# Denominators of the first five tiles of the second pass on POOL, during the second group of G; the other tiles' 1e-6 on ACT

## The chip, the cores and the metric

The kernel runs on one core of one Trainium2 chip. A core has five engines with a queue of instructions each: PE (matrix products and transposes), DVE (vector), ACT (activation functions, copies), POOL (GpSimd) and SP (which here only issues DMAs). Each works off its own queue in order, and an instruction waits at the head of its queue until what it needs is there. The metric is the device time of one execution in microseconds (us), the median of several. Before the change it is 804.62 us (three runs, 804.2 to 806.26).

## The reference

Two layers, each a Fourier mixing sublayer and then a linear attention block, over x of 2048 tokens by 640 features in f32. The input generator stores the DFT matrices, wqkv (640 x 1920) and wo (640 x 640). The part that the change touches is the attention. In the names used below, with 32 heads of 20 features and phi a positive feature map:

```
xn   = layernorm(x)
pq   = phi(xn @ wq);  pk = phi(xn @ wk);  v = xn @ wv
kv_h = sum over tokens of pk_h^T v_h          (20 x 20 for each head)
z_h  = sum over tokens of pk_h                (20 for each head)
o_h  = (pq_h @ kv_h) / (pq_h . z_h + 1e-6)
x    = x + concat(o_h) @ wo
```

`pq_h . z_h + 1e-6` is one number for each token and head, the denominator: 32 for each token, 128 x 32 for a tile of 128 tokens.

## The kernel before

x stays in SBUF as 16 tiles X of 128 tokens by 640 features. Products that need more precision than one fast pass are split: `split` makes a high part (a cast on ACT, L134) and a low part (a subtraction on DVE, L135), and PE adds three products.

Attention runs in two passes over the tokens. The first is `keys_values`. For each tile it normalizes x (`norm`, DVE, L128 or L124), transposes it, and computes keys pk and queries pq with phi on ACT (L284 to L286) and DVE (L287). POOL adds up all keys in `pksum` (L299). The values are never computed for each token: instead G = sum of xn^T pk (640 x 640, only the parts needed) is gathered in PSUM, and kv follows as wv^T G. G is gathered in two groups of tokens, tiles 0 to 9 and, after all keys are there, tiles 10 to 15 (`CUT` is 10). For each tile `gram_ready` norms x again, and splits xn and pk (two casts on ACT, two low parts on DVE); the low part of the keys is called w in the trace, that of xn t. `gram` then runs 30 products (L252), five of which share a chunk of features: high times high, high times low, low times high. Work of tile n+1 is made ready while PE is at tile n.

After the first tile of the second group, `total` (L360) multiplies pksum with a matrix of ones on PE, which leaves z, summed over all tokens and copied to all 128 partitions, in spare columns of G's banks. In the kernel before, `total_out` copies z to SBUF (`zb`, three copies on ACT, L369 and L370) when the whole second group is done. In layer 0 the same stage runs pieces of a check that compares loaded constants (DVE, L1047 and L1064, called junk); in layer 1 there are none.

`combine` adds both groups of G (L350, DVE), computes kv (L400), masks it (L409), and multiplies each of six blocks of kv by wo (`rows`, L168 on PE), which gives the matrix M of the second pass. In the same stretch the first tiles of the second pass are prepared: `weigh(n)` multiplies pq and zb on POOL (L444, 128x640) and `weighted(n)` finishes on DVE: a reduction over the 20 features of each head (L457), + 1e-6 (L458), the reciprocal (L459), and pq times the reciprocal in two instructions (L461 with 600 columns, L467 with 40).

`outputs` is the second pass. For each tile n of `order2`: POOL multiplies for tile n+3, five transposes (L140) for tile n+1, `weighted` for tile n+2, 60 products with M (L168), the split of the next tile's transposed weighted queries (L134, L135), and the residual (L500, DVE). In layer 0 this pass also feeds the next layer's Fourier sublayer, tile by tile: statistics and norms on ACT (L112, L113, L126) with scalars on POOL (L114, L115, L118), and folds of tokens on POOL (L748, L749, L753) and DVE (L764 and on). In layer 1 it stores the output instead.

Temporaries of 128 x 640 come from a pool of 12 buffers (`temp`), PSUM has four buffers of two banks. The order of instructions on each engine is set at build time by a scheduler that takes priorities, which the table `AHEAD` moves for named pieces ('0weigh0' is tile 0's `weighted` in layer 0). What waits for what is then fixed; the order in which instructions stand in each queue is part of the program. The engine orders of the two kernels differ only from the second group of G to the end of the second pass in each layer, on PE, DVE, ACT and POOL; SP's order is the same.

Of the kernel before, what the change touches and what calls it, by code (L numbers as in the profile page):

```python
# [8 lines left out]
F32 = mybir.dt.float32  # L9
F32R = mybir.dt.float32r  # L10
AF = mybir.ActivationFunctionType
ALU = mybir.AluOpType
AX = mybir.AxisListType

S, D, H, DH = 2048, 640, 32, 20
# [30 lines left out]
VLOWS = (0, 0, 1, 0)  # L46
WLOWS = ((5, 2), (1, 1))
GATE = 2
AHEAD = {'0out00': -60, '2keep00': -60, '2out10': -600, '1q13': 60, '2keep01': 600, '2keep02': 5, '0kv0': 5, '2out02': -20, '0out10': -600, '0keep00': -5, '1q14': 60, '0w1': 5, '2out01': 20, '0kv2': -600, '0m1': -5, '0kv5': 60, '1weigh15': -20, '0out12': -200, '1res13': 5, '2m1': -20, '0keep10': 60, '0weigh0': 60, '0first': -5, '2out12': -200, '2weigh1': 5, '2first': 60, '0m3': 20, '2out13': -200}


class K:
    def __init__(self, tc, ctx):
        self.tc, self.nc = tc, tc.nc
        nc = self.nc
        self.n = self.layer = self.part = 0
        self.cst = ctx.enter_context(tc.tile_pool(name="cst", bufs=1))
        self.psp = ctx.enter_context(tc.tile_pool(name="ps", bufs=4, space=bass.MemoryType.PSUM))
        self.ident = self.cst.tile([128, 128], F32, name="ident")
        make_identity(nc, self.ident)  # L60
        self.ones = self.cst.tile([128, 128], F32, name="ones")
        nc.vector.memset(self.ones, 1.0)
        self.mhalf = self.cst.tile([128, 1], F32, name="mhalf")
        nc.vector.memset(self.mhalf, -0.5)

# [89 lines left out]
def h2(t):  # L155
    return t.rearrange("p (a b) -> p a b", a=2)
# [16 lines left out]
class Attention:  # L173
    def __init__(self, k, X, order, order2, wqkv, wo, mask, saved=None):
        self.k, self.X, self.order, self.order2, self.mask, self.saved = k, X, order, order2, mask, saved
        self.wqkv, self.wo, self.W = wqkv, wo, {}
        self.kept = {}

    def wt(self):
        return self.k.wp.tile([128, 640], F32R, tag="w", name=self.k.nm("w"))  # L180
# [83 lines left out]
    def keys_values(self, check=None, keep=1, saves=()):  # L264

        saves = list(saves)
        k, nc, W = self.k, self.k.nc, self.W
        pksum = k.temp()
        nc.gpsimd.memset(pksum, 0.0)
        self.PQ, late = {}, []  # L270
        if check is not None:
            check.fetch()

        def proj(part, x, mid=None):
            pu = k.psum()
            for cs in (range(ND),) if mid is None else (range(2), range(2, ND)):
                product(nc, pu, *x, [w[0] for w in W[part]], [w[1] for w in W[part]], cs=cs)
                if mid is not None and cs[0] == 0:
                    mid()
            return pu  # L280

        def phi(pu, out):
            e = k.temp()
            nc.scalar.activation(h2(e), halves(pu), AF.Relu, scale=-1.0)  # L284
            nc.scalar.activation(h2(out), halves(pu), AF.Relu)
            nc.scalar.activation(e, e, AF.Exp, scale=-1.0)  # L286
            nc.vector.scalar_tensor_tensor(out, e, 1e-6, out, op0=ALU.add, op1=ALU.add)  # L287

        x, acc, tail = self.x0, [], None
        for a, b in ((0, CUT), (CUT, NT)):  # L290
            pks = []
            for n in range(a, b):
                with k.ahead("normed", n + 1):
                    xn = self.normed(n + 1) if n + 1 < NT else None
                pk = self.slot()
                pu = proj(1, x)
                with k.ahead("key", n):
                    phi(pu, pk)
                nc.gpsimd.tensor_tensor(pksum, pksum, pk, op=ALU.add)  # L299
                pks.append(pk)  # L300
                def chunks(xn=xn, n=n):
                    tp = k.transposed(xn)
                    with k.ahead("chunks", n):
                        return k.split_chunks(tp)

                def query(i=self.order[n], x=x, mid=None):
                    pq = k.pqp.tile([128, D], F32, tag="pq", name=k.nm("pq"))
                    pu = proj(0, x, mid)
                    with k.ahead("query", i):
                        phi(pu, pq)  # L310
                    self.PQ[i] = pq

                got = []
                if xn is not None and n:
                    got.append(chunks())
                if n < NT - keep:
                    query(mid=None if got or xn is None else lambda: got.append(chunks()))
                else:
                    late.append(query)
                if n in SAVES[0] and saves:  # L320
                    self.save(*saves.pop(0))
                if check is not None and n in STEPS[0]:
                    check.step(True)
                if n == b - 2:
                    with k.ahead("gram", a):
                        ready = self.gram_ready(a, pks[0])
                if xn is not None:
                    x = got[0]
            G = [k.psum() for _ in range(3)]
            tail = tail or k.psum()  # L330
            for n in range(a, b):
                with k.ahead("gram", n + 1):
                    nxt = self.gram_ready(n + 1, pks[n + 1 - a]) if n + 1 < b else None
                self.gram(G + [tail], ready, n == a, n == b - 1, a == 0)
                if n in SAVES[1] and saves:
                    self.save(*saves.pop(0))
                if n == CUT:
                    self.total(G, pksum)
                if check is not None and n in STEPS[1]:
                    check.step(n != STEPS[1][-1])  # L340
                ready = nxt
            if a == 0:
                acc = [self.slot() for _ in range(ND)]
                for c in range(ND):
                    (nc.scalar.copy if c % 2 else nc.vector.tensor_copy)(acc[c][:, :GA], self.place(G, c, 0))
                nc.scalar.copy(acc[ND - 1][:, GA:], self.place(G, ND - 1, 1))
        assert not saves
        self.total_out(G)
        for c in range(ND):
            nc.vector.tensor_tensor(acc[c][:, :GA], acc[c][:, :GA], self.place(G, c, 0), op=ALU.add)  # L350
        c = ND - 1
        nc.vector.tensor_tensor(acc[c][:, GA:], acc[c][:, GA:], self.place(G, c, 1), op=ALU.add)
        for c in range(ND - 1):
            nc.scalar.copy(acc[c][:, GA:], self.place([None] * 3 + [tail], c, 1))
        self.combine(acc, late)
# [16 lines left out]
    def combine(self, G, late):  # L372
# [65 lines left out]
            self.M.append(m)  # L438
        self.next, self.t1 = qd, self.weigh(2)

    def weigh(self, n):
        k = self.k
        t1 = k.temp()
        k.nc.gpsimd.tensor_tensor(t1, self.PQ[self.order2[n]], self.zb, op=ALU.mult)  # L444
        return t1

    def weighted(self, n, t1):

        k, nc, pq = self.k, self.k.nc, self.PQ[self.order2[n]]
        heads = lambda t: t.rearrange("p (h d) -> p h d", d=DH)
        den, rden = (
            k.sm.tile([128, H], F32, tag="sm" + n, name=k.nm(n), bufs=2) for n in ("den", "rden")
        )
        nc.vector.tensor_reduce(den, heads(t1), axis=AX.X, op=ALU.add)  # L457
        nc.vector.tensor_scalar(den, den, 1e-6, None, op0=ALU.add)  # L458
        nc.vector.reciprocal(rden, den)  # L459
        chunks = t1.rearrange("p (i c) -> p i c", i=ND)  # L460
        nc.vector.tensor_tensor(  # L461
            chunks[:, :, :EC].rearrange("p i (h d) -> p i h d", d=DH),
            pq[:, : EC * ND].rearrange("p (i h d) -> p i h d", i=ND, d=DH),
            rden[:, : 6 * ND].rearrange("p (i h) -> p i h", i=ND).unsqueeze(3).to_broadcast([128, ND, 6, DH]),
            op=ALU.mult,
        )
        nc.vector.tensor_tensor(  # L467
            chunks[:, :, EC:].rearrange("p i (h s) -> p h i s", h=2),
            pq[:, EC * ND :].rearrange("p (h i s) -> p h i s", h=2, i=ND),
            rden[:, 6 * ND :].unsqueeze(2).unsqueeze(3).to_broadcast([128, 2, ND, 4]),  # L470
            op=ALU.mult,
        )
        return t1

    def outputs(self, after, between=lambda: None):
# [4 lines left out]
        for n, i in enumerate(self.order2):  # L480
# [16 lines left out]
            for pu, hs in zip(pus, parts):  # L497
# [3 lines left out]
                after(i, hs[0], hs[-1] + 1)  # L501
            if n == NT - GATE:
                late = last
# [854 lines left out]
```

## Time and profile before

| | us |
|---|---|
| median of three runs | 804.62 (804.2 to 806.26) |
| the profiled execution | 805.39 |
| its span, first to last instruction | 803.5 |
| mean granted TensorE clock | 0.992 |

The stages that the change touches, in the profiled execution, from busy time by stage:

| stage | layer 0 | layer 1 |
|---|---|---|
| second group of G, from the total on | 293.27 to 316.55 | 677.40 to 699.10 |
| kv, rows of M, first tiles weighed | 316.55 to 365.00 | 699.10 to 724.85 |
| outputs | 365.00 to 422.60 | 724.85 to 803.50 |

The first stage of layer 0 begins with the total (to 294.65), that of layer 1 after it. In layer 0 the transposes and products of the first tiles of the second pass run within the second stage.

How to read the rows: a row of the timeline is start, length, engine, line, operation, output, inputs, shape and count, and in brackets the idle time before it and what ended it. A group row has busy time of all, the mean of one in ns, and the idle time before. A wait row is who waited for whom: us in total, times, longest. PEld is PE's loading of weights beside its products. Line numbers are those of the kernel before; in the changed kernel the same lines stand some lines further down (L252 becomes L255, L135 becomes L138, L168 becomes L171).

### The profile page before, as it was taken

The page shows a single profiled execution, that of the slowest core. Times are in us where ns is not written, and L with a number is a line of the kernel's source. Part 1 is how long each engine was busy: PE and PEld are TensorE (multiplying, and loading weights), DVE is VectorE, ACT ScalarE, POOL GpSimd, SP SyncE. Part 2 cuts the span into 40 slices and gives each one's busy share as a digit, 9 for nine tenths or more (in the row PEclk, how much of TensorE's full clock was granted, in tenths as well). Part 3 has the DMA queues.
Part 4 walks back from the last instruction along what each step waited for, and adds up shares of the span by engine and source line. Part 5 has one row for each costly group of instructions (what it writes and reads, how often), then busy time and mean ns, then how long its engine had stood idle before and what let it go on. Part 6 is the DMA issues. An engine that isn't in the chain of part 4 may idle for free.

```text
span 803.5 us, 12981 instructions
## 1 busy us (share of the span) xinstructions
PE 744.2 (93%) x4920; PEld 706.5 (88%) x4920; DVE 612.6 (76%) x1153; ACT 337.7 (42%) x592; POOL 317.7 (40%) x354
## 2 busy tenths in 40 slices
PE   0579999999999999999898999999999999999997
PEld 0138899999999999899784899999999999989997
DVE  7799883778774775989978787377896398499982
ACT  4534544545324553455552434445532455341110
POOL 4987991111021111369894756111101111134310
PEclk9989999999999999999999999999999999999999
DMA  9122430455770452000004551044444044001121
GB/s 329 57 86 66 134 101 1 143 162 175 215 229 15 153 179 78 21 1 2 0 1 145 202 204 48 1 142 142 142 142 141 1 142 144 20 12 50 66 84 70
DMA packets 36008, 81.25 MB, mean 101 GB/s; under 512 B 4142, under 2 KB 5937, under 8 KB 35936
## 3 DMA queue, kind: packets, MB, share of 16 engines
q1 hardware_dynamic: 35904, 80.27, 30.9%
q8 instruction: 41, 0.67, 0.3%
q14 instruction: 31, 0.25, 0.1%
q0 software_dynamic: 32, 0.06, 0.0%
HBM read 68.10 MB, written 11.80 MB: 99 GB/s over the span
## 4 chain that ended last, share of the span: by engine, by line
PE 64%; DVE 21%; POOL 5%; DMA 3%; ACT 3%; issue 3%; SPq 0%; DVEq 0%; POOLq 0%; ACTq 0%
PE ps L168 44%; PE ps L252 13%; PE ps L140 3%; PE ps L947 3%; DVE w L135 2%; DVE t L135 2%; DVE junk L1064 1%; DMA ck<-in_ck 1%; DVE x L974 1%; DVE den L457 1%; POOL ab L623 1%; DVE t L461 1%; PE ps L400 1%; DMA rawc<-in_so 1%; DMA x<-in_x 1%
## 5 line engine op out<-in xcount | busy, mean ns | idle before, releaser
L168 PE MATMUL ps<-w,t 128*128 128x320 f32 x2880 | 440.2, 311 | 7.7 <-DVE t L135 5.7
L168 PEld LDWEIGHTS ps<-w,t 128*128 128x128 f32 x2880 | 422.8, 188 | 10.9 <-DVE t L135 7.7
L299 POOL TENSOR_TENSOR t<-t,s 128x640 f32<-128x640 f32 x32 | 58.3, 1822 | 219.3 <-DVE s L287 211.8
L252 PE MATMUL ps<-t,t 128*128 128x256 f32 (+1 forms) x640 | 139.9, 309 | 0.0
L284 ACT ACTIVATE t<-ps 128x640 f32<-128x640 f32 x64 | 45.2, 705 | 156.3 <-PE ps L168 156.3
L252 PEld LDWEIGHTS ps<-t,t 128*128 128x128 f32 x640 | 107.3, 188 | 0.0
L1064 DVE CUSTOM_DVE_ANT_0 junk<-ck,ck 128x688 bf16<-128x688 f32 (+4 forms) x138 | 98.6, 714 | 7.3 <-DMA ck<-in_ck 5.5
L252 PE MATMUL ps<-w,t 128*128 128x384 f32 (+1 forms) x320 | 98.7, 310 | 0.7 <-DVE w L135 0.6
L444 POOL TENSOR_TENSOR t<-pq,t 128x640 f32<-128x640 f32 x32 | 56.1, 1758 | 101.3 <-ACT t L370 48.5
L135 DVE TENSOR_TENSOR t<-ps,t 128x640 fp32r<-128x640 f32 (+1 forms) x66 | 53.8, 817 | 41.3 <-ACT t L134 41.0
L134 ACT CAST t<-ps 128x640 fp32r<-128x640 f32 (+1 forms) x66 | 45.6, 692 | 67.3 <-PE ps L140 63.1
L902 PE MATMUL ps<-cw,ab 128*107 128x512 f32 (+4 forms) x108 | 42.8, 533 | 33.0 <-DVE ab L643 26.1
L287 DVE SCALAR_TENSOR_TENSOR pq<-t,pq 128x640 f32<-128x640 f32 x32 | 27.6, 861 | 54.3 <-ACT t L286 54.3
L902 PEld LDWEIGHTS ps<-cw,ab 128*107 128x107 f32 (+1 forms) x108 | 18.5, 183 | 51.8 <-issue 47.7
L252 PEld LDWEIGHTS ps<-w,t 128*128 128x128 f32 x320 | 60.1, 188 | 1.5 <-DVE w L135 1.5
L947 PE MATMUL ps<-t,u 107*128 107x322 f32 (+1 forms) x306 | 48.9, 315 | 2.6 <-DVE t L135 1.4
L947 PEld LDWEIGHTS ps<-t,u 107*128 107x128 f32 (+1 forms) x306 | 45.8, 189 | 5.0 <-DVE u L928 2.2
L286 ACT ACTIVATE t<-t 128x640 f32<-128x640 f32 x64 | 48.0, 750 | 0.0
L140 PE MATMUL ps<-ident,t 128*128 128x128 f32 x320 | 45.6, 273 | 1.5 <-DVE t L467 1.0
L128 DVE TENSOR_SCALAR t<-x,kept 128x640 f32<-128x640 f32 x58 | 44.4, 766 | 0.7 <-PE ps L252 0.7
L140 PEld LDWEIGHTS ps<-ident,t 128*128 128x128 f32 x320 | 38.3, 140 | 3.2 <-issue 1.5
L134 ACT CAST t<-t 128x640 fp32r<-128x640 f32 x32 | 23.3, 729 | 36.6 <-DVE t L128 31.8
(178 smaller groups left out, 999.4 us busy)
## 6 DMA issues: line engine op xcount, KB each, us to landing
ck<-in_ck SPq DMA_DIRECT2D x48, 346.0 KB
ck<-in_ck SPq DMA_DIRECT2D x48, 344.0 KB
save<-w SPq DMA_DIRECT2D x20, 320.0 KB
w<-save SPq DMA_DIRECT2D x20, 320.0 KB
x<-in_x SPq DMA_DIRECT2D x16, 320.0 KB
out<-x SPq DMA_DIRECT2D x15, 320.0 KB
raw<-in_wqkv SPq DMA_DIRECT2D x10, 320.0 KB
s<-in_wqkv SPq DMA_DIRECT2D x10, 320.0 KB
```

Source lines behind the costliest of these rows:

```text
L134: self.nc.scalar.copy(hi, src)
L135: self.engine(pool).tensor_tensor(lo, src, hi.bitcast(F32), op=ALU.subtract)
L140: self.nc.tensor.transpose(tp[:, 128 * c : 128 * c + 128], src[:, 128 * c : 128 * c + 128], self.ident)
L168: nc.tensor.matmul(pu[:m, 512 * h : 512 * h + HD], s, w[:, HD * h : HD * h + HD], start=first, stop=last)
L252: nc.tensor.matmul(self.place(G, c, part), x[:, 128 * c : 128 * c + 128], p[:, f : f + n], start=start and i == 0, stop=stop and i == 2, s ...
L284: nc.scalar.activation(h2(e), halves(pu), AF.Relu, scale=-1.0)
L286: nc.scalar.activation(e, e, AF.Exp, scale=-1.0)
L299: nc.gpsimd.tensor_tensor(pksum, pksum, pk, op=ALU.add)
L444: k.nc.gpsimd.tensor_tensor(t1, self.PQ[self.order2[n]], self.zb, op=ALU.mult)
L902: nc.tensor.matmul(pu[:m, o : o + n], e, w[:, f : f + n], start=g == 0 and i == 0, stop=g == end and not more and i == len(both) - 1,)
L947: self.k.nc.tensor.matmul(po[:, o : o + 322], s[:m, f : f + 128], w[:m, x, :], start=first, stop=last)
L1064: i = nc.vector.tensor_tensor_reduce(k.junk[:, : a.shape[1]], b, a, 1.0, 0.0, op0, op1, o)
```

## The change

Four things are done. A constant tile of 1e-6 is made. `total_out` is called directly after `total`, within the second group, and no longer after it. `denominators` follows it: for the first five tiles of the second pass (whose queries are all there) POOL multiplies pq and zb, sums the 20 products of each head by four additions that halve the columns (10, 5, 2, 1) and a last one of columns 0 and 4, and adds 1e-6: seven instructions a tile, 35 a layer, in two temporaries by turns and one tile for the 5 x 32 results. `weigh` gives those tiles only a temporary, and `weighted` starts with the reciprocal. For the eleven other tiles the reduction stays on DVE and 1e-6 is added by ACT.

```diff
+EARLY = 5
...
+        self.eps = self.cst.tile([128, 1], F32, name="eps")
+        nc.vector.memset(self.eps, 1e-6)
...
                 if n == CUT:
                     self.total(G, pksum)
+                    self.total_out(G)
+                    self.denominators()
...
         assert not saves
-        self.total_out(G)
...
+    def denominators(self):
+
+        k, nc = self.k, self.k.nc
+        t1 = [k.temp() for _ in range(2)]
+        all_den = k.sm.tile([128, H * EARLY], F32, tag="early", name=k.nm("early"), bufs=1)
+        for n in range(EARLY):
+            if self.order2[n] in self.PQ:
+                self.early(n, all_den[:, H * n : H * n + H], t1[n % 2])
+
+    def early(self, n, den, t1):
+        k, nc = self.k, self.k.nc
+        nc.gpsimd.tensor_tensor(t1, self.PQ[self.order2[n]], self.zb, op=ALU.mult)
+        self.den[n] = den
+        t = t1.rearrange("p (h d) -> p h d", d=DH)
+        for w, o in ((10, 10), (5, 5), (2, 2), (1, 1)):
+            nc.gpsimd.tensor_tensor(t[:, :, :w], t[:, :, :w], t[:, :, o : o + w], op=ALU.add)
+        nc.gpsimd.tensor_tensor(den, t[:, :, 0], t[:, :, 4], op=ALU.add)
+        nc.gpsimd.tensor_scalar(den, den, 1e-6, None, op0=ALU.add)
+
     def weigh(self, n):
         k = self.k
         t1 = k.temp()
+        if n in self.den:
+            return t1
         k.nc.gpsimd.tensor_tensor(t1, self.PQ[self.order2[n]], self.zb, op=ALU.mult)
         return t1
...
-        nc.vector.tensor_reduce(den, heads(t1), axis=AX.X, op=ALU.add)
-        nc.vector.tensor_scalar(den, den, 1e-6, None, op0=ALU.add)
+        if n in self.den:
+            den = self.den[n]
+        else:
+            nc.vector.tensor_reduce(den, heads(t1), axis=AX.X, op=ALU.add)
+            nc.scalar.activation(den, den, AF.Identity, bias=k.eps)
         nc.vector.reciprocal(rden, den)
```

In the changed order on DVE the reciprocals of tiles 0 and 1 stand among the splits of tiles 14 and 15 of the second group, and those of tile 2 ahead of the additions of G. On POOL the instructions of tiles 0 and 1 alternate, then those of 2 and 3, then tile 4's follow; tile 2's product stands ahead of tile 1's last addition. On PE twelve short products of tile 11 now stand ahead of the total.

More of the change, by code (lines that the diff above doesn't have):

```diff
@@ L176, in __init__ @@
         self.wqkv, self.wo, self.W = wqkv, wo, {}
-        self.kept = {}
+        self.kept, self.den = {}, {}
     def wt(self):
```

## The prediction

> **What bounds the kernel now.** I read the page first, then the chain of waits around the second group of G, then busy time by stage, then the groups by line.
>
> ```profile
> span 803.5 us, 12981 instructions
> PE 744.2 (93%) x4920; PEld 706.5 (88%) x4920; DVE 612.6 (76%) x1153; ACT 337.7 (42%) x592; POOL 317.7 (40%) x354
> PE 64%; DVE 21%; POOL 5%; DMA 3%; ACT 3%; issue 3%; SPq 0%; DVEq 0%; POOLq 0%; ACTq 0%
> ```
>
> PE is busy 93% of the span, so only places where PE waits can pay, and every new PE wait costs. The chain, layer 0, over the stage that the change fills (start, length, work):
>
> ```profile
> 291.21 2.01 POOL t L299
> 293.22 0.04 issue
> 293.27 1.38 PE ps L360 x10
> 294.65 21.90 PE ps L252 x149
> 316.55 4.41 PE ps L168 x30
> ```
>
> The last sum of keys on POOL releases the total, then PE runs the 150 products of tiles 11 to 15 of the second group (4.38 us a tile) without a gap. The stages (window and length; then busy us of PE, PEld, DVE, ACT, POOL):
>
> ```profile
> 293.27:316.55 23.28, 23.28 (x161) 23.28 (x162) 14.06 (x27) 9.02 (x18) 0.00 (x0) 1.00 0.25 76
> 335.64:365.00 29.36, 29.26 (x205) 29.01 (x205) 26.96 (x46) 14.52 (x30) 19.06 (x27) 1.00 0.03 9
> 365.00:422.60 57.60, 51.55 (x348) 48.96 (x346) 51.16 (x75) 30.44 (x61) 52.31 (x71) 1.00 0.01 2
> 677.40:699.10 21.70, 21.70 (x151) 21.70 (x149) 9.92 (x15) 8.46 (x17) 0.00 (x0) 1.00 0.20 60
> 699.10:724.85 25.75, 24.00 (x177) 21.53 (x176) 25.73 (x51) 10.11 (x21) 12.03 (x7) 1.00 0.05 10
> 724.85:803.50 78.65, 73.05 (x516) 72.70 (x514) 60.00 (x96) 9.72 (x14) 16.00 (x10) 0.98 0.18 69
> ```
>
> In G (rows 1 and 4) PE is full and POOL is idle: that is the room the change uses. In layer 0's outputs (row 3) PE idles 6.05 us with DVE and POOL both near 90%. In layer 1's outputs (last row) PE sets the pace.
>
> **Part 1: 35 POOL instructions in each G.** Prices, from the groups by line (busy in all, mean ns):
>
> ```profile
> L444 POOL TENSOR_TENSOR t<-pq,t 128x640 f32<-128x640 f32 x32 | 56.1, 1758 | 101.3 <-ACT t L370 48.5 <-PE ps L168 26.9 <-DVE w L135 6.4
> 385.54 0.18 POOL L749 COPY ab<-t 128x2 f32<-128x2 f32 x1
> 385.68 0.87 POOL L753 TENSOR_TENSOR ab<-t 128x319 f32<-128x319 f32 x1
> L791 POOL TENSOR_TENSOR ab<-ab,ab 128x640 f32<-128x640 f32 x3 | 4.7, 1568 | 0.1
> ```
>
> 640 elements take 1.57 us undisturbed, 319 take 0.87, two take 0.18: (1.57 − 0.87)/321 = 2.2 ns an element over 0.17. The adds of 320, 160, 64 and 32 elements, and the last of 32, then take 0.87, 0.52, 0.31, 0.25 and 0.25, the 1e-6 0.19; with the product 1.57 that is 3.96 us a tile and 20 us a layer. No row has adds of this stride (20 apart). The bounds: 0.17 each, the part that does not grow with the size (1.5 less for each tile), and twice the price (2.4 more). I take the single price, which all four rows above support for f32 operands of their sizes.
>
> 20 us would fit under 21.9 if POOL ran beside DVE. It does not, and this is the step that decides:
>
> ```profile
> 290.98 0.82 DVE L135 TENSOR_TENSOR t<-t,t 128x640 fp32r<-128x640 f32 x1
> 291.21 2.00 POOL L299 TENSOR_TENSOR t<-t,s 128x640 f32<-128x640 f32 x1 [6.58 <-DVE s L287]
> 291.72 1.85 DVE L128 TENSOR_SCALAR t<-x,kept 128x640 f32<-128x640 f32 x1
> 295.16 0.61 DVE L128 TENSOR_SCALAR t<-x,kept 128x640 f32<-128x640 f32 x1
> ```
>
> The POOL product that started inside a DVE split took 2.00 instead of 1.57 (it ended 1.41 after the split), and the norm behind it took 1.85 where one with POOL idle takes 0.61: each waits for the other's whole instruction. What DVE has to do in G is just of that kind:
>
> ```profile
> L135 DVE TENSOR_TENSOR t<-t,t 128x640 fp32r<-128x640 f32 x32 | 26.3, 821 | 12.7 <-ACT t L134 12.2
> 296.66 0.87 DVE L1064 CUSTOM_DVE_ANT_0 junk<-ck,ck 128x692 bf16<-128x692 f32 x1
> 301.95 0.70 DVE L1064 CUSTOM_DVE_ANT_0 junk<-ck,ck 128x519 bf16<-128x519 f32 x1
> 303.83 0.33 DVE L1064 CUSTOM_DVE_ANT_0 junk<-ck,ck 128x173 bf16<-128x173 f32 x1
> 304.78 0.82 DVE L135 TENSOR_TENSOR t<-t,t 128x640 fp32r<-128x640 f32 x1 [0.62 <-ACT t L134]
> 305.53 0.82 DVE L135 TENSOR_TENSOR w<-s,t 128x640 fp32r<-128x640 f32 x1
> L369 ACT COPY t<-ps 128x256 f32<-128x256 f32 x4 | 1.6, 411 | 0.0
> ```
>
> Splits follow each other 0.75 apart (304.78, 305.53), 0.07 under what one lasts, and I take as much off the norm and the check pieces. I write t(n) and w(n) for the low parts of tile n's norm and keys, x(n) for its norm. In the new order PE does twelve products of tile 11 before the total (256 columns each, so some 1.4 us, under 12 × 0.147). They start when w(11) lands, which follows POOL's last sum (ended 293.22) and takes 0.74: 293.95. The total (1.38) then ends near 296.75, and ACT's copies of z, which follow it bank by bank (0.41, 0.41 and a shorter one), near 297.2. The splits of tile 12 on ACT stand behind these copies. Alone that is a delay of 0.8 us. From 297.2 on POOL runs. Up to w(14) and with it the new DVE order has six splits (t and w of tiles 12, 13 and 14: 4.5 us), x(13) and x(14) (1.1), five check pieces in layer 0 (three at 0.80, then 0.63 and 0.26: 3.3) and the reciprocals of early tiles 0 and 1. These two wait for POOL, which interleaves tiles 0 and 1 and slips in tile 2's product: 3 × 1.57 + 2 × 2.39 = 9.5. One after the other: 297.2 + 8.9 + 9.5 + 0.4 for the reciprocals and 0.5 for hops from ACT (0.62 at 304.78) = 316.5 for w(14), where PE wants it at 316.55 − 2 × 4.38 = 307.8. Then two tiles of PE: G ends at 325.3, **+8.7** at strict alternation. In layer 1 there are no check pieces. Z lands 2.55 after the stage's start, as in layer 0 (297.2 after 294.65), at 680.0; DVE has 5.6 and the first reciprocal's 0.2, POOL 9.3: w(14) at 695.1, wanted at 699.10 − 8.76 = 690.3: **+4.8**.
>
> Alternation is not quite strict. A stretch of layer 0's outputs with both busy:
>
> ```profile
> 384.09 0.77 DVE L461 TENSOR_TENSOR t<-pq,rden 128x600 f32<-128x600 f32 x1
> ...
> 387.89 0.83 DVE L766 TENSOR_TENSOR ab<-ab,ab 128x640 f32<-128x640 f32 x1
> 387.99 1.44 POOL L753 TENSOR_TENSOR ab<-t 128x319 f32<-128x319 f32 x1
> ```
>
> Between 384.09 and 389.43 twelve operations, 6.4 us at undisturbed prices, pass in 5.3: 0.1 saved a handoff. With two handoffs for each of thirteen DVE operations up to w(14) in layer 0 and of eight in layer 1: 8.7 − 2.6 = **+6.1**, 4.8 − 1.6 = **+3.2**. Bounds: +0.8 and +0.3 when DVE's slack (w(15) was ready at 306.35, five microseconds early) swallows the rest, +13.5 when strict.
>
> By the Trainium skill ("SBUF — State Buffer", section "SBUF: two separate sides"), the port pair that VectorE and GpSimd share is an exclusive lock, held for a whole instruction when VectorE reads two SBUF inputs or runs a two-port mode, and the loser fully blocks. The trace agrees in kind (1.85 against 0.61), and by that rule the strict sum would hold.
>
> **Part 2: what outputs get back.** DVE loses the addition of all sixteen tiles (eleven go to ACT) and the reduction of five:
>
> ```profile
> L457 DVE TENSOR_REDUCE den<-t 128x32 f32<-128x640 f32 x32 | 25.6, 804 | 0.6 <-POOL t L444 0.6
> L458 DVE TENSOR_SCALAR den<-den 128x32 f32<-128x32 f32 x7 | 3.6, 521 | 0.0
> 384.01 0.15 DVE L458 TENSOR_SCALAR den<-den 128x32 f32<-128x32 f32 x1
> PE ps L168 <- DVE t L135: 4.8, 4, 2.1
> PE ps L168 <- ACT t L134: 1.0, 2, 0.7
> 724.12 0.73 PE L140 MATMUL ps<-ident,t 128*128 128x128 f32 x5 [0.96 <-DVE t L467]
> ```
>
> Row 2 is the stage from 365 to 422.6 of layer 0: seven additions, 3.6 us, of which 0.15 each is work (row 3) and the rest waiting for POOL. That waiting goes partly to the next instruction (the product, which waits for POOL too). So between 1.0 and 3.6, and never above PE's idle 5.8 (rows 4 and 5); POOL, at 52.31 of 57.60, also limits it. I take −2.4. The stage before, with the early tiles 3 and 4, has PE at 29.26 of 29.36: nothing. In the stage of the products of rows I take −0.4 in layer 0, half of one reduction (0.80), since the early tiles' reductions there are gone and PE runs nearly without a gap; in layer 1 the wait at 724.12, −0.7 of 0.96. Layer 1's outputs: nothing, DVE has 18 us to spare. Sum **−3.5** (0 to −6.5).
>
> ACT's addition is one more hop.
>
> ```profile
> ACT t L126 <- POOL mv L118: 13.0, 7, 3.0
> L112 ACT ACTIVATION_READ_ACCUMULATOR t<-x 128x1 f32 x17 | 3.2, 187 | 0.0
> ```
>
> Nothing on ACT has its size; a read of one element takes 0.19 (row 2), a copy of 256 columns 0.41 (above), so 0.2 to 0.4, and DVE's queue has another tile's instruction between reduction and reciprocal, which covers it; uncovered it would be 0.4 a tile on a chain that has slack in layer 1 and none in the stage from 365. It can also be late where it stands behind a statistic that waits for POOL (row 1). Seven waits, up to 3.0: in the new order the additions of tiles 8, 9, 11 and 12 stand behind one. Zero taken, up to +3 for the range. The memset of 1e-6 runs at the start beside loads: nothing. SP's queue keeps its order.
>
> The rest of part 1: two temporaries are held through G, so ACT's query of the late tile waits for tile 3's adds and a mask for tile 4's; the reciprocal of tile 2 stands ahead of G's additions and waits for POOL to about 297.2 + 16 + 10.5 = 323.7, before 325.3: covered by the same delay.
>
> **Sum** on the profiled execution, 805.39: +6.1 + 3.2 − 3.5 = +5.8, so 811.2; against the median 804.62 (0.77 lower) **810.5**.
>
> **Rivals.** *DVE's slack holds* (the other side). Place: w(14) of both layers. If POOL's short adds let DVE pass at once, DVE waits mostly for pieces of 0.2 to 0.5 and G is late by 0.8 to 3 in all, while outputs give 3.5 to 6.5: 799.5 to 804, 802 as its middle. It decides once G's two delays sum to under 3.5. For it: DVE is 14.06 busy of 23.28 in G, and 5 us early. Against: the reciprocals in DVE's queue make w(14) wait for POOL's whole two trees, whichever engine is served first. *Strict alternation*: no handoff saves anything, G costs +13.5: 805.39 + 10.0 − 0.77 = 814.6. For it: the norm's 1.85; against: the twelve operations in 5.3. *Strided adds cost twice.* Each tree is 2.4 us dearer, two of them ahead of w(14), twice: +8 to +9, 819. For it: no row has them. Against: rows of POOL go by element count. *The ACT addition is late* behind the waiting statistics: part 2's −2.4 goes and up to 3 comes: 814 to 816. *The denominators are not done within G*: 20 us of POOL after 297.2 do not fit before 316.55 with DVE's 11 in between; but what then waits (tile 2's reciprocal, above) lands within the delay already counted, so it gives the forecast.
>
> **How the numbers follow.** Forecast (with the last rival) 0.42, 810.5, own range 806 to 815; strict alternation 0.10; slack holds 0.30; adds twice 0.10; late addition 0.08. No change is within 0.3%, 802.2 to 807.0, about what a measurement tells. Slack splits 0.17 faster and 0.13 same; the forecast leaves 0.05 same. So faster 0.17, same 0.18, slower 0.65. The range leaves out the best of the slack and the worst of doubled adds: 801.5 to 818.
>
> **What would show it.** In the new profile: POOL busy about 20 us in each second group of G; x(13), x(14) and the splits there at 1.2 to 2.3 instead of 0.61 and 0.82; PE waiting in L255's products for w(14) or the splits; G's last product about 6 later in layer 0 than before, counted from the total, and 3 later in layer 1. In the outputs PE's waits for the low split falling from 4.8 to 2 to 3, the wait at 724.12 gone. I am wrong if G shows no PE wait, if the adds take over 1.5 times their price, or if PE waits in the outputs grow.

## The result, and the profile after

The changed kernel takes 812.26 us (median of four runs, 811.15 to 814.65) against 804.72 us for the kernel before (four runs): a ratio of 1.0095, 95% interval 1.0083 to 1.0107. It is slower, 1.8 us above the 810.5 forecast and inside its range of 801.5 to 818. The profiled execution is the fastest of the four, 811.15 us with a span of 809.4, and that of the kernel before lies 0.7 above its median. So the profiles, from which all stages below are taken, show 5.9 us of the 7.5 by which the medians differ.

The page of the changed kernel: the span, busy time of the engines, and the chain of waits by engine.

```profile
span 809.4 us, 13016 instructions
PE 746.8 (92%) x4920; PEld 708.0 (87%) x4920; DVE 602.6 (74%) x1112; ACT 344.1 (43%) x614; POOL 358.8 (44%) x414
PE 63%; DVE 18%; POOL 11%; ACT 3%; issue 3%; DMA 1%; SPq 0%; ACTq 0%; POOLq 0%; DVEq 0%
```

DVE has 10.0 us less to do, POOL 41.1 more (two layers of 20), and POOL's share of the chain went from 5% to 11%. The chain of waits of the changed kernel in layer 0, around the second group of G (start, length, work) shows where; some steps marked "issue", all under 0.3 us, are left out:

```profile
291.35 2.00 POOL t L302
293.35 3.83 issue
...
297.22 3.66 POOL t L456 x2
300.88 7.69 POOL t L460 x8
308.57 0.99 POOL early L461 x2
309.63 0.33 POOL early L462
309.99 0.04 DVE rden L487
310.26 1.56 DVE junk L1092
311.82 0.01 DVE cm L1092
311.82 0.77 DVE t L138
312.59 0.07 DVE rden L487
312.78 1.90 DVE w L138
314.72 8.46 PE ps L255 x56
323.19 4.40 PE ps L171 x30
```

Before, that stretch of the chain was PE alone: 150 products without a gap. Now it runs through POOL's products and adds (L456, L460 to L462) for 12.7 us, a reciprocal (L487), a check piece, and the low parts t(14) and w(14) on DVE; only then come PE's last 56 products of G. Z was in SBUF at 297.2, as worked out; w(14) landed at 314.7 (worked out at strict alternation: 316.5). PE's four waits in that group, from the timeline of the changed kernel, are for w(11), w(12), w(13) and w(14):

```profile
294.09 0.40 PE L255 MATMUL ps<-w,t 128*128 128x256 f32 x1 [1.20 <-DVE w L138]
301.62 0.39 PE L255 MATMUL ps<-w,t 128*128 128x256 f32 x1 [1.15 <-DVE w L138]
307.99 0.39 PE L255 MATMUL ps<-w,t 128*128 128x256 f32 x1 [1.61 <-DVE w L138]
314.72 0.39 PE L255 MATMUL ps<-w,t 128*128 128x256 f32 x1 [2.10 <-DVE w L138]
```

Busy time by stage of the changed kernel (window, length, then PE, PEld, DVE, ACT, POOL): the second group of layer 0 and that of layer 1.

```profile
293.35:323.19 29.84, 24.24 (x161) 23.26 (x162) 23.19 (x33) 8.67 (x18) 25.32 (x31) 1.00 0.16 47
679.99:706.30 26.31, 24.13 (x161) 23.20 (x162) 18.55 (x21) 8.64 (x18) 21.96 (x28) 1.00 0.18 54
```

DVE and POOL together show 48.5 us busy in 29.84 us of layer 0's G: as the stretched instructions below show, the busy time of both contains time in which one waits for the other.

To place the difference I cut each execution at the same events: the start of POOL's last sum of keys, the first product of the rows of M, the residual (L500 before, L528 after) of the first tile, that of the last tile. Busy time by stage between these cuts, for the rows of M and for the outputs of layer 0, first before, then after:

```profile
316.39:341.71 25.32, 23.92 (x178) 22.01 (x177) 25.05 (x53) 10.83 (x22) 11.58 (x6) 1.00 0.09 21
341.71:424.94 83.23, 75.65 (x514) 72.66 (x513) 73.70 (x114) 44.85 (x89) 70.54 (x97) 1.00 0.03 9
```

```profile
323.02:346.97 23.95, 22.96 (x175) 21.34 (x174) 19.28 (x40) 11.03 (x22) 6.14 (x7) 1.00 0.14 34
346.97:430.46 83.49, 78.24 (x518) 74.99 (x517) 68.92 (x99) 47.67 (x100) 73.38 (x97) 0.98 0.03 10
```

| stage, us | before | after | difference |
|---|---|---|---|
| start to POOL's last sum, layer 0 | 291.21 | 291.35 | +0.14 |
| G, layer 0 | 25.18 | 31.67 | +6.49 |
| rows of M and first products, layer 0 | 25.32 | 23.95 | −1.37 |
| outputs, first to last residual, layer 0 | 83.23 | 83.49 | +0.26 |
| Fourier and first pass of layer 1 | 249.02 | 247.52 | −1.50 |
| G, layer 1 | 25.14 | 28.16 | +3.02 |
| the rest of layer 1 | 104.40 | 103.26 | −1.14 |
| span | 803.5 | 809.4 | +5.9 |

A residual is an instruction of DVE, so the number of products that PE has done by the first one varies: 178 before, 175 after, and 170 to 185 in the experiments. A product is worth 0.147 us (75.65 for 514), so the rows of M and the outputs should be read together or by PE's idle time, which is the length less PE's busy time.

### The profile page after: what moved, and what is told of

It reads as the page before. It is cut to its first block, busy times and chain, and to the rows that moved or that the text cites. A ratio compares the mean times of both kernels' runs of the same rounds, so it can differ in the third digit from the quotient of the medians.

```text
span 809.4 us, 13016 instructions
## 1 busy us (share of the span) xinstructions
PE 746.8 (92%) x4920; PEld 708.0 (87%) x4920; DVE 602.6 (74%) x1112; ACT 344.1 (43%) x614; POOL 358.8 (44%) x414
## 4 chain that ended last, share of the span: by engine, by line
PE 63%; DVE 18%; POOL 11%; ACT 3%; issue 3%; DMA 1%; SPq 0%; ACTq 0%; POOLq 0%; DVEq 0%
PE ps L171 42%; PE ps L255 11%; PE ps L143 3%; PE ps L975 3%; DVE t L138 2%; POOL t L460 2%; PE ps L404 1%; PE ps L930 1%; POOL ab L651 1%; DVE x L1002 1%; DVE junk L1092 1%; DVE w L138 1%; POOL t L456 1%; ACT t L137 1%; DVE t L131 1%
## 5 line engine op out<-in xcount | busy, mean ns | idle before, releaser
L1092 DVE CUSTOM_DVE_ANT_0 junk<-ck,ck 128x688 bf16<-128x688 f32 (+4 forms) x138 | 100.7, 730 | 5.6 <-DMA ck<-in_ck 3.9
L469 POOL TENSOR_TENSOR t<-pq,t 128x640 f32<-128x640 f32 x22 | 35.1, 1598 | 63.1 <-PE ps L171 33.5
L138 DVE TENSOR_TENSOR t<-t,t 128x640 fp32r<-128x640 f32 x32 | 30.3, 947 | 17.2 <-ACT t L137 17.0
```

Source lines behind the costliest of these rows:

```text
L138: self.engine(pool).tensor_tensor(lo, src, hi.bitcast(F32), op=ALU.subtract)
L1092: i = nc.vector.tensor_tensor_reduce(k.junk[:, : a.shape[1]], b, a, 1.0, 0.0, op0, op1, o)
```

## The experiments

All times are medians, with the ratio to the kernel before from the same chip and its 95% interval. The stages are those of the table above, from one profiled execution each; differences are to the kernel before. "G0" and "G1" are G in layers 0 and 1.

| kernel | ratio (interval) | G0 | rows, layer 0 | outputs, layer 0 | G1 |
|---|---|---|---|---|---|
| changed kernel | 1.0095 (1.0083 to 1.0107) | +6.49 | −1.37 | +0.26 | +3.02 |
| e1_move_only | 0.9974 (0.9961 to 0.9988) | +0.74 | −0.41 | −2.79 | +0.84 |
| e2_act_only | 0.9983 (0.9971 to 0.9994) | +0.01 | +1.12 | −2.60 | +0.09 |
| e3_dve_eps | 1.0098 (1.0083 to 1.0112) | +6.47 | −1.36 | +0.86 | +2.98 |
| e4_small | 1.0018 (1.0005 to 1.0031) | +4.88 | −2.00 | +0.33 | +1.51 |
| e7_recip_late | 1.0031 (1.0020 to 1.0041) | +4.06 | −1.37 | +0.32 | +2.18 |
| e8_small_late | 0.9962 (0.9950 to 0.9975) | +0.73 | −1.69 | −0.42 | +0.82 |
| e9_copy_late | 0.9963 (0.9951 to 0.9975) | −0.05 | −0.40 | −2.48 | +0.07 |
| e10_two_late | 1.0032 (1.0020 to 1.0045) | −0.04 | +0.71 | −1.66 | +0.01 |
| e12_copy_late_dve | 0.9994 (0.9984 to 1.0004) | −0.05 | −2.22 | +1.04 | +0.14 |
| e14_small_late_pool | 1.0035 (1.0021 to 1.0048) | +4.28 | −1.63 | +0.63 | +1.37 |

**e1: everything but the early denominators.**

```diff
                     self.total(G, pksum)
                     self.total_out(G)
-                    self.denominators()
```

> The changed kernel without the early denominators: z is still copied right after the total and the 1e-6 of all sixteen tiles is added on ACT. Theory (the two engines alternating in G cost the time, not the move): G's last product, counted from the last sum of keys on POOL, comes 1 us later than before in layer 0 and under 1 in layer 1, and the outputs give back 1 to 2.5, so 803 to 806. Rival (the moved copies, which stand ahead of ACT's splits, and the twelve products ahead of the total cost it): G 3 to 6 later in each layer, 808 to 813.

Measured 802.96 us. G is 0.74 and 0.84 later: the price of the moved copies and of the products ahead of the total, which the prediction had put at 0.8 and 0.3. The time lies just under the theory's range. The rest of G's delay belongs to the early denominators.

**e2: the 1e-6 on ACT alone**, in the kernel before.

```diff
-        nc.vector.tensor_scalar(den, den, 1e-6, None, op0=ALU.add)
+        nc.scalar.activation(den, den, AF.Identity, bias=k.eps)
```

> The kernel before, with only the 1e-6 of all tiles moved from DVE to ACT. Theory (DVE's addition is in the way in layer 0's outputs, and the hop to ACT is covered): 802 to 804, the gain in the stage from 365 to 422.6 of layer 0. Rival (the addition is late on ACT behind statistics that wait for POOL): 806 to 809.

Measured 803.49 us, in the theory's range. Layer 0's outputs are 2.60 shorter, the rows of M 1.12 longer, but the second figure is where the cut falls. Busy time by stage of e2_act_only, rows of M and outputs:

```profile
315.26:341.70 26.44, 25.31 (x185) 22.89 (x184) 26.44 (x49) 12.46 (x27) 10.89 (x6) 1.00 0.09 20
341.70:422.33 80.63, 75.83 (x506) 73.98 (x506) 66.84 (x101) 47.73 (x100) 71.93 (x97) 0.96 0.03 10
```

DVE comes to the first residual later, and by then PE has done seven products more; it idles 1.13 in the rows, before 1.40. So the additional hop costs PE nothing there. Both stages together are 1.48 shorter. PE's idle time in the outputs fell by 2.78, from 7.58 to 4.80.

**e4: early instructions cut in size**, with the chain of waits kept.

```diff
-        nc.gpsimd.tensor_tensor(t1, self.PQ[self.order2[n]], self.zb, op=ALU.mult)
+        nc.gpsimd.tensor_tensor(t1[:, :32], self.PQ[self.order2[n]][:, :32], self.zb[:, :32], op=ALU.mult)
...
-            nc.gpsimd.tensor_tensor(t[:, :, :w], t[:, :, :w], t[:, :, o : o + w], op=ALU.add)
-        nc.gpsimd.tensor_tensor(den, t[:, :, 0], t[:, :, 4], op=ALU.add)
+            nc.gpsimd.tensor_tensor(t1[:, :2], t1[:, :2], t1[:, 2:4], op=ALU.add)
+        nc.gpsimd.tensor_tensor(den, t1[:, :32], self.zb[:, :32], op=ALU.add)
```

> The changed kernel with all 35 early POOL instructions of a layer in the same order and with the same chain of waits, but cut in size: the products take 32 columns, the adds two columns, the last one 32. The denominators of tiles 0 to 4 are left out. Theory (what counts is how long POOL holds DVE up): POOL's time in G falls from 20 us to under 8, G's last product comes 1 to 2.5 later than before in layer 0 and 0.3 to 1.5 in layer 1 instead of 6.5 and 3.2, and the outputs give the same back as the changed kernel: 801.5 to 805. Rival (number of instructions, their handoffs and the waits of the reciprocals count, not the sizes): 809 to 812.

Measured 806.86 us, between the two. In layer 0 G was still 4.88 late, though POOL's instructions were short, so the length of POOL's instructions was not all that held G up. The scheduler had placed things differently too: in this kernel norms and splits of later tiles got buffers that the early temporaries had held. The timeline of e4_small, a norm on DVE with the idle time before it:

```profile
304.76 0.61 DVE L131 TENSOR_SCALAR t<-x,kept 128x640 f32<-128x640 f32 x1 [1.39 <-POOL early L461]
```

**e7: reciprocals behind G.** Full-size early work; the reciprocals of the early tiles are ordered after G's last addition.

```diff
+        self.added = nc.vector.tensor_tensor(acc[c][:, GA:], acc[c][:, GA:], self.place(G, c, 1), op=ALU.add)
...
+        first = nc.vector.reciprocal(rden, den)
+        if n in self.den:
+            k.after(first, self.added)
```

> The changed kernel with the reciprocals of the early tiles held until after G's last addition, so that no instruction of DVE in G waits for a result of POOL; POOL's work and DVE's order are otherwise the same. Theory (DVE and POOL exclude each other on SBUF): G is late by 5 to 6.5 in layer 0 and 2.5 to 3.2 in layer 1 as before, 811 to 813.5. Rival (DVE waits in its queue for POOL's trees): G is late by at most 2 and 1, 804 to 807.

Measured 807.40 us: G 4.06 and 2.18 later, where the changed kernel has 6.49 and 3.02. So 2.43 and 0.84 come from the reciprocals in DVE's queue; this lies between the two expectations. PE waits for w(11), w(12) and w(13) as in the changed kernel (1.20, 1.15 and 1.59), and the wait for w(14) is gone. The timeline of e7_recip_late on DVE shows the rest. No instruction of DVE here waits for a POOL result:

```profile
297.73 1.67 DVE L138 TENSOR_TENSOR t<-t,t 128x640 fp32r<-128x640 f32 x1 [3.22 <-ACT t L137]
299.32 2.17 DVE L138 TENSOR_TENSOR w<-s,t 128x640 fp32r<-128x640 f32 x1
301.66 1.22 DVE L1094 CUSTOM_DVE_ANT_0 junk<-ck,ck 128x692 bf16<-128x692 f32 x1
302.82 1.08 DVE L131 TENSOR_SCALAR t<-x,kept 128x640 f32<-128x640 f32 x1
303.82 1.21 DVE L1094 CUSTOM_DVE_ANT_0 junk<-ck,ck 128x692 bf16<-128x692 f32 x1
304.97 1.16 DVE L138 TENSOR_TENSOR t<-t,t 128x640 fp32r<-128x640 f32 x1
```

Undisturbed these take 0.82, 0.82, 0.87, 0.61, 0.87 and 0.82. These six alone are 3.7 us over.

**e8: small, late, with buffers of their own.** The small instructions of e4, the order of e7, and `t1` from a pool of its own:

```diff
-        t1 = [k.temp() for _ in range(2)]
+        t1 = [k.sm.tile([128, 32], F32, tag="own%d" % u, name=k.nm("own"), bufs=1) for u in range(2)]
```

> As the run with small early instructions, but their two temporaries have buffers of their own, so that no other temporary waits for them, and the reciprocals stand behind G's last addition as in the run with late reciprocals. The denominators of tiles 0 to 4 are left out. Same number of POOL instructions, almost no time of POOL in each. Theory (the length of POOL's instructions holds DVE up): G is late by 0.5 to 1.5 in each layer, 801.5 to 805. Rival (each handoff costs, whatever the size): G late by 3 to 4 in layer 0, 806 to 808.

Measured 802.20 us, with G 0.73 and 0.82 later, which is what e1 pays without any early instruction. The same count of POOL instructions, at these sizes, adds nothing to G beyond what e1 pays. The groups by line of e8_small_late on POOL and on DVE, in the second group of layer 0:

```profile
L459 POOL TENSOR_TENSOR own<-own 128x2 f32<-128x2 f32 x20 | 7.6, 407 | 0.3
L461 POOL TENSOR_SCALAR early<-early 128x32 f32<-128x32 f32 x5 | 2.8, 564 | 0.4
```

```profile
L138 DVE TENSOR_TENSOR w<-s,t 128x640 fp32r<-128x640 f32 x4 | 3.4, 842 | 0.0
L1093 DVE CUSTOM_DVE_ANT_0 junk<-ck,ck 128x692 bf16<-128x692 f32 x3 | 2.7, 885 | 0.0
L131 DVE TENSOR_SCALAR t<-x,kept 128x640 f32<-128x640 f32 x3 | 1.9, 619 | 0.0
```

A low part w takes 0.84 here. The same view of the changed kernel, on DVE:

```profile
L138 DVE TENSOR_TENSOR w<-s,t 128x640 fp32r<-128x640 f32 x4 | 6.1, 1528 | 0.0
L1092 DVE CUSTOM_DVE_ANT_0 junk<-ck,ck 128x692 bf16<-128x692 f32 x3 | 3.4, 1136 | 0.0
L487 DVE RECIPROCAL rden<-early 128x32 f32<-128x32 f32 x3 | 1.0, 348 | 2.1 <-POOL early L462 2.1
```

1.53 instead of 0.84 for w, and three reciprocals that waited 2.1 in all.

**e14: small, late, in the common pool.** It is e8 with the temporaries where e4 has them.

```diff
-        t1 = [k.sm.tile([128, 32], F32, tag="own%d" % u, name=k.nm("own"), bufs=1) for u in range(2)]
+        t1 = [k.temp() for _ in range(2)]
```

> The small early instructions with the reciprocals behind G's last addition, and the two temporaries in the common pool of temporaries again. The denominators of tiles 0 to 4 are left out. It differs from one earlier run in the reciprocals alone, from another in the buffers alone, from the run with late reciprocals in the sizes alone. Theory (with small instructions, what made G 4.9 late in layer 0 was that norms and splits of tile 14 waited for buffers that POOL held until its last tiles): G late by 2 to 4 in layer 0, 804 to 806. Rival (it was the reciprocals): G late by under 1.5, 802 to 803.5.

Measured 806.63 us, 0.6 over what the theory allowed for the whole, with G 4.28 late in layer 0, a little over its 2 to 4. Against e8 (buffers alone) that is 3.55 more; against e4 (reciprocals alone) 0.60 less. So most of e4's delay was the buffers. The view of waits of e14_small_late_pool in G names them (who waited for whom, us, times, longest):

```profile
DVE t L131 <- POOL early L461: 1.8, 1, 1.8
DVE t L138 <- POOL early L461: 1.6, 1, 1.6
```

Neither of these waits stands in the changed kernel or in e7, where the scheduler gave those buffers out otherwise; there, of waits for POOL's early results, only the reciprocals' show. By its edit e14 differs from e7 in the sizes alone, and there the small sizes take the stretching away (the mean of the splits t in G is 0.84 against 1.35, of the norms 0.61 against 1.04), yet G is no earlier (4.28 against 4.06), because the two waits for buffers, 3.4 in all, came in its place. No version with full-size instructions and buffers of their own was run, so no pair of runs gives the price of the sizes with all else equal.

**e3: the changed kernel with the other tiles' 1e-6 on DVE.**

```diff
-            nc.scalar.activation(den, den, AF.Identity, bias=k.eps)
+            nc.vector.tensor_scalar(den, den, 1e-6, None, op0=ALU.add)
```

> The changed kernel with the 1e-6 of the eleven other tiles added on DVE again, as before; the five early denominators stay on POOL. Theory (what the outputs give back, 2.6 us in layer 0 and 1.1 in layer 1, comes from the additions that went to ACT): most of it is gone, 813.5 to 816. Rival (it comes from the five tiles whose reduction left DVE and from the earlier copies of z): 811 to 813.

Measured 812.58 us: the rival. Beside the early denominators, the additions on ACT are worth 0.60 in layer 0's outputs (+0.86 against +0.26) and nothing that the whole time shows.

**e9 and e12: copies of z three tiles later**, no early denominators; e9 with the 1e-6 on ACT, e12 on DVE.

```diff
                 if n == CUT:
                     self.total(G, pksum)
+                if n == CUT + 3:
                     self.total_out(G)
-                    self.denominators()
```

> The run without early denominators (z copied within G, 1e-6 of all tiles on ACT), with the three copies of z made three tiles later, when ACT's splits for G are nearly done. Theory (of the 0.8 that G lost in each layer there, the copies ahead of the splits and the delayed total took it): G is late by at most 0.3, the rest as there, 800.5 to 802.5. Rival (twelve products ahead of the total come from the scheduler in any case): 802.5 to 804.

> As the run with late copies of z and no early denominators, but 1e-6 added on DVE as in the kernel before: only the place of the three copies of z is changed. Theory (copying z within G lets POOL multiply and DVE reduce the first tiles inside G, and the additions on ACT shorten layer 0's outputs; each gives a part): 802.5 to 804, the outputs of layer 0 as long as before. Rival (the whole gain is in ACT's additions): 804 to 805.5; or (the whole gain is in the copies): 801.5 to 802.5.

e9 measured 802.21 us, in the theory's range, with G as before in both layers. Of the versions that compute the whole output it has the lowest ratio (0.9963, 0.9951 to 0.9975), faster than both kernels at hand; the intervals of e1 and e2 overlap with its own. With the copies three tiles later, among ACT's last splits, nothing of G is lost. In its timeline POOL's first two products of the second pass run within G, when DVE is at its last split:

```profile
307.91 3.57 POOL L469 TENSOR_TENSOR t<-pq,t 128x640 f32<-128x640 f32 x2 [15.40 <-ACT t L374]
```

e12 measured 804.22 us, no difference from before that can be told, and in the range of the first rival, that the gain is in ACT's additions. e9 and e12 differ only in the addition. In the rows PE idles 0.6 in both (0.61 and 0.59), though DVE comes to the first residual 1.82 later in e9; in the outputs it idles 4.32 in e9 and 5.87 in e12. Rows and outputs together are 1.70 shorter with the addition on ACT. The profiled execution of e12 is the slowest of its eleven (806.65): the rest of layer 1 is 2.28 longer than before in it, with a granted clock of 0.83 between 725 and 732 us, where the kernel before has 1.00.

**e10: two early denominators, late copies, late reciprocals.** `EARLY = 2`, `denominators` at the fifth tile of the second group, `k.after` as in e7.

> The same with two early denominators a layer (tiles 0 and 1), begun by POOL only after the late copies of z, when DVE has done most of G's splits, and with their reciprocals behind G's last addition. Theory (POOL is free of cost where DVE is idle in G): G late by at most 0.5 a layer and the first products of the second pass not later, 800 to 803. Rival (two fewer reductions bring nothing, and POOL's trees still hold up the last splits): 803 to 806.

Measured 807.37 us, above both ranges. The theory's first half holds: G is not late at all (−0.04 and +0.01), although POOL runs two full-size trees in it, because DVE is at its last split when they begin. The rows of M are 1.1 longer than in e9, and the rest of layer 1 took 108.0 against 104.1. Of these 3.9 us, 2.15 are longer busy time of PE for the same 690 products, and 1.74 more idle time. In its profile the granted clock was 0.76 between 725 and 732 us, where that of e9 and of the kernel before is 1.00, and the last product of the comparison of constants (L1122 on PE) waited 2.6 for DVE, 1.0 longer than in e9. Why the clock fell in this program is open.

## Why the prediction came out right

Forecast 810.5 (the working gives 811.2 less 0.77, which is 810.4), measured 812.26 against a base of 804.72. By the profiled executions the sum was +5.8, and the span grew by 5.9. That this agrees to 0.1 is partly luck: the returns did not come where the prediction had them, and the medians differ by 7.5. Point by point:

1. **G, +6.1 and +3.2.** Measured +6.49 and +3.02. The mechanism holds: DVE's splits, norms and check pieces take turns with POOL's instructions, whose length decides. This is read from the stretched instructions (w 1.53 in the changed kernel, 0.84 in e8), from e10, where trees of full size beside an idle DVE cost G nothing, and from e7 against e8, 3.33 and 1.36 (not sizes alone, since e8's temporaries have their own buffers, but e7 shows no wait for a buffer that POOL holds). The shares found are, in layer 0, 0.74 for the move (e1), some 3.3 for taking turns and 2.43 for the reciprocals in DVE's queue (e7 against the changed kernel); in layer 1 0.84, 1.3 and 0.84. The prediction had counted all in one chain up to w(14), in which the reciprocals wait for two whole trees "whichever engine is served first". In fact PE already waits for w(11), w(12) and w(13), and the reciprocals carry a bit over a third of the delay in layer 0 (2.43 of 6.49). The rival *DVE's slack holds* is wrong even without the reciprocals: e7's two delays sum to 6.24, over the 3.5 that was to decide. Strict turns would have been +8.7 and +4.8. The 0.1 that the prediction takes off for each handoff is an average over one stretch of outputs, and not all of it is turns: the reciprocal in that stretch (0.33 of the 1.1 saved) is not stretched beside POOL.

2. **The price of the early work**, 20 us a layer. It holds. The timeline of the changed kernel on POOL has these, worked out as 0.87, 0.52 and 1.57; below them is what DVE did at the same time, the additions of G, which read one operand from PSUM:

```profile
322.96 0.82 POOL L460 TENSOR_TENSOR t<-t 128x320 f32<-128x320 f32 x1
323.85 0.54 POOL L460 TENSOR_TENSOR t<-t 128x160 f32<-128x160 f32 x1
320.94 1.57 POOL L456 TENSOR_TENSOR t<-pq,t 128x640 f32<-128x640 f32 x1
321.63 2.41 DVE L354 TENSOR_TENSOR s<-s,ps 128x384 f32<-128x384 f32 x5 [0.39 <-PE ps L255]
```

   These additions have a median of 0.55 in both kernels, so here neither engine is stretched. Nor is a reciprocal, 0.34 in the middle of a POOL product (312.52 in the changed kernel). So it is not every instruction of DVE that takes turns with POOL; those seen to do so have all their tensors in SBUF. With DVE idle, in e10, the eight adds of two trees take this:

```profile
311.52 3.48 POOL L462 TENSOR_TENSOR t<-t 128x320 f32<-128x320 f32 x8
```

   It was worked out as 3.90. So *strided adds cost twice* is out. What makes them longer in the chain above is DVE's splits beside them.

3. **What outputs get back, −2.4.** The size came out, the place did not. PE's idle time in layer 0's outputs fell by 2.33, from 7.58 to 5.25. But its wait for the low split, forecast to fall from 4.8 to 2 to 3, is still 4.6. What went are other waits of PE, 1.0 for ACT's high parts and 1.5 for a DMA (the first two rows are the waits of the kernel before in its outputs, the third of the changed kernel):

```profile
PE ps L902 <- DMA cw<-in_co: 1.5, 1, 1.5
PE ps L168 <- ACT t L134: 1.0, 2, 0.7
PE ps L171 <- DVE t L138: 4.6, 4, 2.1
```

   So this step failed as a mechanism, and that the idle time fell by 2.33 is luck; no run settles why these two waits went. Without early denominators the wait for the low split does fall, to 3.1, 2.7 and 2.3 (e1, e2, e9); why not beside them is open, since the order of that stage differs in many places. And the stage is not shorter, but 0.26 longer, because PE's busy time in it grew by 2.59. Four more products lie between the cuts, which is 0.6. The other 2.0 are slower products: 0.151 each, before 0.147, and most of it lies here, where the granted clock was 0.67 and 15 products took 3.80:

```profile
400.00:405.00 5.00, 3.80 (x15) 3.80 (x16) 5.00 (x7) 1.89 (x4) 4.84 (x7) 0.67 0.00 0
```

   The prediction's sum has no term for a change of the clock. In e3, with the five early tiles and the additions on DVE, PE's idle time in this stage is 6.83, so the additions on ACT are worth 1.58 of the 2.33.

4. **Where the return came from.** The whole return is −3.75, forecast −3.5. From the first product of the rows to layer 1's last sum of keys it is −2.61 (forecast −2.8). The rows of M are 1.37 shorter; 0.41 of that is idle time of PE, as forecast (−0.4), the rest busy time, three products of it (0.44) because the cut falls earlier. The stretch from the last residual to layer 1's G is 1.50 shorter; e3, e4, e7, e8 and e14, all with five early tiles, have it at 247.2 to 247.9, and the runs without them, or with two, at 248.6 to 249.1. That was not forecast. PE idles 3.50 there instead of 4.48, and a wait of 0.8 for DVE (L800) is gone; why is open. The rest of layer 1 gave 1.14 (forecast 0.7): the wait at 724.12 is gone, as forecast, but a new one of 1.05, for a low part on DVE, stands at 723.21.

5. **ACT's addition.** It takes 0.32, inside the bounds of 0.2 to 0.4. "Zero" for the hop was right, in outputs and between G and the rows: in the outputs of the changed kernel DVE never waits for it, and PE idles no longer in the rows of e2 than before.

6. **The rest**: copies and total 0.74 where 0.8 was worked out in layer 0; 0.84 against 0.3 in layer 1.

## What to carry to other kernels

An engine that is idle in a stage is not free if its instructions take turns with those of the engine that feeds the bound: some 20 us of POOL work under 24 us of PE work stretched DVE's splits from 0.84 to 1.53, and this put some 3.3 of the 6.5 us on the path. The same kind of work, two trees of it, cost G nothing when it began at DVE's last split (e10). Where a result is queued matters as much as when it is computed: an instruction that waits for it must not stand ahead of work that PE needs, and the buffers it holds must not be those that this work asks for next. The part of such a change that pays can be small: here copying z within G, but late in it, and moving one addition to ACT gain 0.37% with none of the early work. And where stages are compared between kernels, the length alone misleads when a cut lies on another engine or the clock differs; PE's idle time and its number of products tell the two apart.

## What the runs showed that was not expected

A 128x2 addition on POOL has a mean of 0.41 us in e8, and took POOL 7.6 us for twenty: small instructions next to a busy DVE are stretched too, but do not stretch it (w 0.84). In the outputs of layer 0 of the changed kernel the granted clock fell to 0.67 between 400 and 405 us, after a PE wait of 2.09 (the row is in point 3 above); the kernel before, with a longest wait of 2.1 too, has 1.00 in every slice of this stage. Every other profiled execution has such a fall within this stage, e9 down to 0.50 in the same slice of time. So the fall does not set e9 apart from the changed kernel, but it does hide part of what each variant gained over the profile of the kernel before. One profiled execution of each cannot tell whether it belongs to the program or to the execution.
